# The order of the first loads in a fused attention and rational feed-forward kernel: small transfers set between large ones, two more pieces of the first weight ahead of values and queries

## The chip, the cores and the metric

The kernel runs on one core of a Trainium2 chip. The metric is device time in microseconds (us) of one execution: the median of three runs is compared. Besides, one execution is recorded by the hardware profiler; its times are counted from the start of its span.

## What is computed

Attention through 32 packed queries `p` per head, with 8 batches, 8 heads, 576 rows and a head dimension of 64, and behind it a feed-forward layer with a rational activation, all in 32-bit floats, the weights coming in as 64-bit floats:

```python
p_packed = sm_attn(p, k, v)                 # softmax(p k^T / 8) v, 32 rows for a head
out      = sm_attn(q, p_packed, p_packed)   # softmax(q p_packed^T / 8) p_packed
x = out.transpose(0, 2, 1, 3).reshape(4608, 512)
h = x @ w_in                                # 512 x 2048
P = a0 + a1*h + a2*h**2 + a3*h**3
Q = 1 + |b0|*|h| + |b1|*h**2
result = (P / (Q + 1e-6)) @ w_out           # 2048 x 512
```

## The kernel before

**Weights as words.** `w_in` and `w_out` are 64-bit floats, handed over as 64-bit integers. They come in 16 pieces of 1 MB, which the kernel calls words: eight of `w_in` and eight of `w_out`, each made of 256 of the 2048 inner columns (or rows). Each word is loaded by two transfers of 512 KB. The list `words` (line 369) holds them in the order in which they fall due: words 0 to 5 are of `w_in`, word 6 is the first of `w_out`, and from there the two kinds alternate. `load_words(n)` (line 380) issues loads until n words lie loaded and not yet converted, as far as buffers are free; a word lies in one of the buffers `m0` to `m3` or `w1` to `w5`. `w2` and `w3` hold values and queries of batch 0 first and are given to words only once the variable `started` is set. `convert()` (line 431) makes 32-bit floats of the next word: two activations on ScalarE (profile: `m<-m` and `win<-m`, or `w<-w` and `win<-w`) and three instructions on VectorE (TENSOR_SCALAR, SCALAR_TENSOR_TENSOR, and an integer addition that the profile calls CUSTOM_DVE_ANT_0 and the list of instructions ISA), each on 128 x 1024 elements. A converted word of `w_in` lies in `win`.

**Loads of a batch.** `load(bb, what)` (line 468) issues the transfers of batch `bb`. For batch 0 they are `k0`, `k1`, `v0`, `v1`, `q0` and `q1` of 512 KB each, one half of the heads' first 512 rows, into the tiles `nat` (keys) and `w2`, `w3` (values, queries), and `rem`, all that is small: the keys' last 64 rows (tile `AH`, 128 KB in rows of 256 bytes), the packed queries (`pn`, four transfers of 16 KB, and a copy of them on GpSimd), the queries' last 64 rows (also `AH`, two of 64 KB) and the values' last 64 rows (`rv`, two of 64 KB). All are issued on SyncE's queue. The four coefficients `a` and two `b` go to the tile `ab` from `constants()` (line 337); from them VectorE computes the tiles `root` and `abS`, and ScalarE loads four registers from `abS` (TENSOR_LOAD).

**Attention of one batch.** `attention(bb)` (line 539) transposes the keys on TensorE (copied to the tile `kx` by ScalarE), takes the packed queries' scores, reduces their maxima on VectorE, exponentiates on ScalarE, transposes the result, multiplies by the values into the tile `acc` (profile, batch 0: `acc<-w,kx` and `acc<-rv,small`), scales that on VectorE (`small<-acc,small`), transposes it to `ppT`, and then lets the queries attend to it. Its output goes to `AH` and `AL`, the high and low parts of a split that lets TensorE keep 32-bit accuracy in three passes.

**Feed-forward.** `m_chunk` multiplies a converted piece of `w_in` by `ppT` ahead of time, so that `hidden` works on attention weights of 128 columns; `hidden(bb, x, c)` computes one unit of h, the rational function (tiles `U`, `V`, `Y` on ScalarE, VectorE and GpSimd) and `gh`, `gl`; `acc_block` multiplies by `w_out` and sums in `acc`. There are 128 units; the first 12 use `w_out` undivided, while words are still being converted.

**What sets the order.** Every call is recorded and not issued: the class `Planner` (line 32) collects the operations, finds their dependencies, and lays them out by list scheduling with a table of costs (a transfer is costed by its size and the length of its contiguous runs). `pin()` gives everything recorded so far the first ranks in the order of recording, so the loads before `nc.pin()` stay as written on SyncE's queue. The order of the other engines is what the planner makes of the whole. `issue` then emits each engine's instructions in that order, and each engine works through its own in order. Where the plan has TensorE idle, `idle` puts multiplications by zero in between (`acc<-w,zero`, profile line 223). All other instructions carry line 226 in the profile, so they are told apart by their tiles.

The lines that the change touches are those of `load` under `what == "rem"` and the start of the program:

```python
load_words(3)
for what in ("k0", "rem", "k1", "v0", "v1", "q0", "q1"):
    load(0, what)
nc.pin()
constants()
```

Of the kernel before, what the change touches and what calls it, by code (L numbers as in the profile page):

```python
# [257 lines left out]
def attention_rational_ffn(  # L258
# [18 lines left out]
    REM = T - NS * P  # L277
# [6 lines left out]
    HREM = REM // 2  # L284
# [35 lines left out]
    pn_ring = Ring(sb, "pn", 1, [P, NG, 2, D])  # L320

    rv_ring = Ring(sb, "rv", 1, [P, H // 2, D])
# [57 lines left out]
    def load_words(n):  # L380
        while len(words_in) < min(len(words), converted + n):
            r = len(words_in)
            kind, i, n2 = words[r]
            used = [x for x, _ in words_in]
            free = [x for x, end in room if r < end and x not in used[converted:]]
            free = [x for x in free if x[0] is not w_ring or x[1] not in (2, 3) or started]
            if not free:
                return
            x = min(free, key=lambda x: max((j for j in range(r) if used[j] == x), default=-1))
            raw = x[0].at(x[1], [P, n2 * 512], I64)  # L390
            if kind == "in":
                c = i // 2
                for y in range(2):
                    src = w_in[2 * y * P : (2 * y + 2) * P, c * CF : (c + 1) * CF].rearrange("(x p) f -> p x f", p=P)
                    nc.sync.dma_start(raw[:, 512 * y : 512 * (y + 1)].rearrange("p (x y) -> p x y", x=2), src)
            else:
                for y in range(n2):
                    nc.sync.dma_start(raw[:, 512 * y : 512 * (y + 1)], w_out[(i + y) * P : (i + y + 1) * P, :])
            words_in.append((x, raw))
# [65 lines left out]
    NAT, AH, AL, PPT = {}, {}, {}, {}  # L465
    rows4 = lambda bb: bb < 2

    def load(bb, what):
        if bb >= B:
            return  # L470
        if what == "rem":

            rv, pn = NAT[bb, "rv"], NAT[bb, "p"] = rv_ring.next(), pn_ring.next()
            if rows4(bb):
                r = NAT[bb, "r"] = AH_ring.at(bb, [P, H, D], F32)
                nc.sync.dma_start(r[0:REM], k[bb, :, NS * P : T, :].rearrange("h p d -> p h d"))
            for j in range(NJ):
                src = p[bb, NG * j : NG * j + NG].rearrange("r n d -> n r d")
                nc.sync.dma_start(pn[32 * j : 32 * j + 32, :, 0, :], src)
            nc.gpsimd.tensor_copy(pn[:, :, 1, :], pn[:, :, 0, :])  # L480
            for i in range(2 if rows4(bb) else 0):
                src = q[bb, 4 * i : 4 * i + 4, NS * P : T, :].rearrange("h (p x) d -> p h (x d)", x=2)
                r2 = r[REM + HREM * i : REM + HREM * (i + 1)].rearrange("p (h x) d -> p h (x d)", x=2)
                nc.sync.dma_start(r2, src)
            for i in range(2):
                src = v[bb, 4 * i : 4 * i + 4, NS * P : T, :]
                if rows4(bb):
                    nc.sync.dma_start(rv[REM * i : REM * (i + 1)], src.rearrange("h p d -> p h d"))
                    continue
                for y in range(2):  # L490
                    o = REM * i + HREM * y
                    nc.sync.dma_start(rv[o : o + HREM], src.rearrange("h (p y) d -> y p h d", y=2)[y])
            return
        x, g = what[0], int(what[1])
        src = {"k": k, "q": q, "v": v}[x][bb, 4 * g : 4 * g + 4]
        if not rows4(bb):
            t = NAT[bb, what] = nat_ring.next()
            if x == "v":
                t = NAT[bb, what] = t[:, 0 : 4 * NS * D].rearrange("p (h s d) -> p h s d", h=4, s=NS)
                for y in range(2):  # L500
                    to = t.rearrange("p h (y i) d -> p h y (i d)", y=2)[:, :, y]
                    nc.sync.dma_start(to, src[:, 2 * P * y : 2 * P * (y + 1)].rearrange("h (p i) d -> p h (i d)", i=2))
                return
            src = src.rearrange("h t d -> (h t) d")
            for i in range(2):
                for y in range(2):
                    o = 64 * i + 32 * y
                    blocks = src[:, 32 * y : 32 * y + 32].rearrange("(a t i) d -> i t a d", t=32, i=2)[i]
                    nc.sync.dma_start(t[o : o + 32].rearrange("p (a d) -> p a d", d=32), blocks)
            return  # L510
        src = src[:, 0 : NS * P, :]
        if bb == 0 and x != "k":
            if g == 0:
                NAT[x] = w_ring.at(2 + "vq".index(x), [P, 2, 4 * NS * D], F32)
            t = NAT[x][:, g, :]
        else:
            t = nat_ring.next()[:, 0 : 4 * NS * D]
        t = t.rearrange("p (h s d) -> p h s d", h=4, s=NS)
        nc.sync.dma_start(t, src.rearrange("h (p s) d -> p h s d", s=NS))
        NAT[bb, what] = t  # L520
# [18 lines left out]
    def attention(bb):  # L539
# [34 lines left out]
        for g in range(2):  # L574
            transposed("k", g)
            if bb > 0:
                load(bb, f"v{g}")
            yield
# [130 lines left out]
        if bb > 0:  # L709
            load(bb, "q0")  # L710
            load(bb, "q1")
# [196 lines left out]
        elif i == 1:  # L908
            nc.sync.dma_start(ov, o)

    load_words(3)
    for what in ("k0", "rem", "k1", "v0", "v1", "q0", "q1"):
        load(0, what)
    nc.pin()
    constants()
    for _ in attention(0):
# [9 lines left out]
    mt, fill, rem = {}, {}, {}  # L926
# [100 lines left out]
```

## Time and profile before

| | |
|---|---|
| median of 3 runs (lowest to highest) | 794.99 us (794.15 to 795.89) |
| the profiled execution, its own time | 795.3 us |
| its span, first to last instruction | 793.2 us |
| granted TensorE clock, mean over the span | 0.975 |
| TensorE busy (matmuls) | 751.6 us, 95% |
| VectorE busy | 698.0 us, 88% |
| ScalarE busy | 662.4 us, 84% |
| GpSimd busy | 453.3 us, 57% |
| moved by DMA | 56.05 MB in 152028 packets |

The profile names TensorE's matmuls PE, its weight loads PEld, VectorE DVE, ScalarE ACT, GpSimd POOL and SyncE's queue SPq. A row of the timeline has the start in us, the length in us, the engine, the line, the operation, the tiles as output<-inputs without buffer numbers, the shapes, the count, and in brackets how long the engine was idle just before and whom it waited for. A row of the stretches has, for each engine, its busy time and in brackets its instructions, then the granted clock of TensorE, the share of the 16 DMA engines and the GB/s. A row of the chain of waits has the start, the length and what the end of the program hung on at that time. A row of the DMA view has the output<-input, the queue, the count, the size of each and the time from issue to landing.

### The profile page before, as it was taken

To read this page: it belongs to the slowest core of one execution; us is meant where nothing else is said; L and a number is where in the kernel's file an instruction comes from. 1 tells how busy PE (TensorE), PEld (TensorE's weight loads), DVE (VectorE), ACT (ScalarE), POOL (GpSimd) and SP (SyncE) were. 2 spreads that over 40 slices of the span, in tenths; PEclk is the share of its full clock that TensorE was granted. 3 is DMA by queue.
4 is the path that set the end of the run, shared out by engine and by line. 5 is a ranking of instruction groups with operands and counts; after the bars stand their busy time and mean duration, and the time that the engine had idled before them with its cause. 6 is when DMAs were issued, how large, how long until landed. Compare 5 with 4: busy or idle time off the path is not lost.

```text
span 793.2 us, 15205 instructions
## 1 busy us (share of the span) xinstructions
PE 751.6 (95%) x5452; PEld 578.9 (73%) x5452; DVE 698.0 (88%) x1298; ACT 662.4 (84%) x1482; POOL 453.3 (57%) x448
## 2 busy tenths in 40 slices
PE   2759999999999999999999999999999999999997
PEld 1436655588778887678777887678777887778886
DVE  4698999998999889998999789998999789998873
ACT  5788979998888888889798798889798798998872
POOL 0012357657576646756587556755587455856663
PEclk9757999999999999999999999999999999999999
DMA  8974326022901038021901138011901122000001
GB/s 268 347 254 162 136 61 87 1 58 49 105 28 54 31 54 114 1 57 43 113 28 52 43 42 116 1 58 46 108 28 50 36 44 56 1 9 20 27 1 41
DMA packets 152028, 56.05 MB, mean 71 GB/s; under 512 B 122256, under 2 KB 141200, under 8 KB 151952
## 3 DMA queue, kind: packets, MB, share of 16 engines
q1 hardware_dynamic: 151952, 55.07, 30.9%
q8 instruction: 43, 0.70, 0.4%
q14 instruction: 33, 0.27, 0.1%
HBM read 45.62 MB, written 9.44 MB: 69 GB/s over the span
## 4 chain that ended last, share of the span: by engine, by line
PE 76%; DVE 10%; ACT 10%; DMA 2%; issue 2%; SPq 1%; POOL 0%; DVEq 0%; ACTq 0%
PE acc L226 38%; PE h L226 23%; PE at L226 14%; DVE Y L226 5%; DVE w L226 2%; ACT Y L226 2%; ACT U L226 1%; DMA AH<-in_k_dram 1%; ACT m L226 1%; ACT kx L226 1%; ACT V L226 1%; ACT sq L226 1%; DVE small L226 1%; DVE V L226 1%; ACT w L226 1%
## 5 line engine op out<-in xcount | busy, mean ns | idle before, releaser
L226 POOL TENSOR_TENSOR U<-U,sq 128x576 f32<-128x576 f32 x128 | 184.9, 1445 | 117.9 <-ACT U L226 54.6
L226 PE MATMUL acc<-w,gh 128*128 128x512 f32 x736 | 237.6, 408 | 1.5 <-ACT gh L226 1.0
L226 PE MATMUL h<-AH,m 128*128 128x288 f32 x1024 | 191.9, 308 | 9.6 <-DVE Y L226 6.9
L226 PEld LDWEIGHTS h<-AH,m 128*128 128x128 f32 x1024 | 158.8, 191 | 41.5 <-DVE Y L226 22.6
L226 POOL TENSOR_TENSOR gl<-Y,gh 128x512 fp32r<-128x512 f32 x116 | 150.1, 1294 | 43.3 <-issue 18.0
L226 PEld LDWEIGHTS acc<-w,gh 128*128 128x128 f32 x736 | 132.1, 188 | 44.8 <-issue 12.2
L226 PE MATMUL acc<-w,gl 128*128 128x512 f32 x384 | 148.1, 413 | 0.7 <-DVE gl L226 0.7
L226 ACT ACTIVATE Y<-h,abS 128x288 f32<-128x288 f32 x256 | 125.9, 507 | 23.1 <-PE h L226 18.9
L226 ACT ACTIVATE sq<-h 128x288 f32<-128x288 f32 x256 | 106.1, 416 | 38.5 <-PE h L226 32.0
L226 DVE TENSOR_TENSOR Y<-Y,h 128x288 f32<-128x288 f32 x256 | 109.6, 446 | 26.0 <-ACT Y L226 9.0
L226 DVE SCALAR_TENSOR_TENSOR Y<-Y,abS,h 128x288 f32<-128x288 f32 x256 | 124.8, 506 | 2.3
L226 DVE SCALAR_TENSOR_TENSOR Y<-Y,abS,V 128x576 f32<-128x576 f32 x128 | 102.9, 804 | 24.1 <-ACT V L226 23.9
L226 PE MATMUL h<-AL,m 128*128 128x288 f32 x512 | 111.0, 298 | 0.0
L226 ACT ACTIVATE U<-h 128x288 f32<-128x288 f32 x256 | 98.3, 419 | 11.5 <-DVE V L226 6.7
L226 ACT ACTIVATE V<-U,one 128x576 f32<-128x576 f32 x128 | 97.9, 765 | 4.8 <-DVE Y L226 4.2
L226 DVE SCALAR_TENSOR_TENSOR V<-U,V 128x576 f32<-128x576 f32 x128 | 96.2, 752 | 0.0
L226 DVE SCALAR_TENSOR_TENSOR Y<-V,Y 128x576 f32<-128x576 f32 x116 | 86.7, 748 | 1.8
L226 PEld LDWEIGHTS acc<-w,gl 128*128 128x128 f32 x384 | 71.5, 188 | 22.7 <-issue 8.8
L226 ACT ACTIVATE V<-V 128x576 f32<-128x576 f32 x128 | 84.2, 658 | 0.6
L226 PEld LDWEIGHTS h<-AL,m 128*128 128x128 f32 x512 | 83.2, 190 | 0.6 <-issue 0.4
L226 POOL COPY G<-Y 128x64 f32<-128x64 f32 x116 | 27.5, 237 | 97.6 <-DVE Y L226 87.0
L226 PE MATMUL acc<-half,gh 128*128 128x512 f32 x240 | 78.6, 414 | 1.1 <-ACT gh L226 1.1
(137 smaller groups left out, 1020.0 us busy)
## 6 DMA issues: line engine op xcount, KB each, us to landing
w<-in_moe_w_out_dram SPq DMA_DIRECT2D x16, 512.0 KB, 4.5
out_dram<-half SPq DMA_DIRECT2D x15, 512.0 KB, 3.1
nat<-in_k_dram SPq DMA_DIRECT2D x48, 144.0 KB, 3.9
nat<-in_q_dram SPq DMA_DIRECT2D x48, 144.0 KB, 4.4
nat<-in_v_dram SPq DMA_DIRECT2D x24, 256.0 KB, 3.4
m<-in_moe_w_in_dram SPq DMA_DIRECT2D x8, 512.0 KB, 6.7
w<-in_moe_w_in_dram SPq DMA_DIRECT2D x8, 512.0 KB, 8.6
nat<-in_k_dram SPq DMA_DIRECT2D x4, 512.0 KB, 10.0
```

What stands on the lines that cost most here:

```text
L226: getattr(getattr(self.nc, engine), name)(*args, **kwargs)
```

## The change

The branch for `rem` in `load` is cut in four, which can be called by themselves: `r` (the keys' last rows), `p` (packed queries with their copy), `qr` (the queries' last rows) and `rv` (the values' last rows). Called as `rem`, for batches 1 to 7, the four go out one after the other; there the two tiles `rv` and `pn` are now made at their own parts. For batch 0 the order is now written as one list, in which a number n stands for `load_words(n)`: words 0 and 1, `r`, word 2, `p`, `k0`, `k1`, `qr`, word 3, `rv`, `v0`, `v1`, word 4, `q0`, `q1`. Before, it was words 0, 1 and 2, `k0`, all of `rem`, `k1`, `v0`, `v1`, `q0`, `q1`, and words 3 and 4 came behind, together with the coefficients. The code behind the loop, `load_words(6)` among it, stands as it was.

```diff
         if what == "rem":
-
-            rv, pn = NAT[bb, "rv"], NAT[bb, "p"] = rv_ring.next(), pn_ring.next()
+            for x in ("r", "p", "qr", "rv"):
+                load(bb, x)
+            return
+
+        if what == "r":
             if rows4(bb):
                 r = NAT[bb, "r"] = AH_ring.at(bb, [P, H, D], F32)
                 nc.sync.dma_start(r[0:REM], k[bb, :, NS * P : T, :].rearrange("h p d -> p h d"))
+            return
+        if what == "p":
+            pn = NAT[bb, "p"] = pn_ring.next()
             for j in range(NJ):
...
             nc.gpsimd.tensor_copy(pn[:, :, 1, :], pn[:, :, 0, :])
+            return
+        if what == "qr":
             for i in range(2 if rows4(bb) else 0):
...
                 nc.sync.dma_start(r2, src)
+            return
+        if what == "rv":
+            rv = NAT[bb, "rv"] = rv_ring.next()
             for i in range(2):
...
-    load_words(3)
-    for what in ("k0", "rem", "k1", "v0", "v1", "q0", "q1"):
-        load(0, what)
+    for what in (2, "r", 3, "p", "k0", "k1", "qr", 4, "rv", "v0", "v1", 5, "q0", "q1"):
+        if isinstance(what, int):
+            load_words(what)
+        else:
+            load(0, what)
     nc.pin()
```

What it moves is seen in the engines' instructions. On SyncE's queue, at the start of the program, stood this before (`m_1` to `m_3` are words 0 to 2, `m_4` and `w_3_119` words 3 and 4; `AH` holds `r` and `qr`, `w_1_84` the values and `w_2_85` the queries):

```order
L226 DMA m_3_78<-in_moe_w_in_dram 128x2x256 x2
L226 DMA nat_1_79<-in_k_dram 128x4x256
L226 DMA AH_1_82<-in_k_dram 64x8x64
L226 DMA pn_1_81<-in_p_dram 32x2x64 x4
L226 DMA AH_1_82<-in_q_dram 32x4x128 x2
L226 DMA rv_1_80<-in_v_dram 64x4x64 x2
L226 DMA nat_2_83<-in_k_dram 128x4x256
L226 DMA w_1_84<-in_v_dram 128x4x256 x2
L226 DMA w_2_85<-in_q_dram 128x4x256 x2
L226 DMA ab<-in_moe_b_dram 128x2
L226 DMA m_4_118<-in_moe_w_in_dram 128x2x256 x2
...
L226 DMA w_3_119<-in_moe_w_in_dram 128x2x256 x2
```

At the same place of SyncE's queue stands now (`m_3_79` is word 2, `m_4_83` word 3 and `w_2_86` word 4, `w_1_85` the values, `w_3_87` the queries):

```order
L226 DMA AH_1_78<-in_k_dram 64x8x64
L226 DMA m_3_79<-in_moe_w_in_dram 128x2x256 x2
L226 DMA pn_1_80<-in_p_dram 32x2x64 x4
L226 DMA nat_1_81<-in_k_dram 128x4x256
L226 DMA nat_2_82<-in_k_dram 128x4x256
L226 DMA AH_1_78<-in_q_dram 32x4x128 x2
L226 DMA m_4_83<-in_moe_w_in_dram 128x2x256 x2
L226 DMA rv_1_84<-in_v_dram 64x4x64 x2
L226 DMA w_1_85<-in_v_dram 128x4x256 x2
L226 DMA w_2_86<-in_moe_w_in_dram 128x2x256 x2
L226 DMA w_3_87<-in_q_dram 128x4x256 x2
L226 DMA ab<-in_moe_b_dram 128x2
```

The nine small transfers (one, four, two and two) no longer stand in a row between `k0` and `k1`; two words, four large transfers, have moved ahead of the queries, and one of the two ahead of the values.

On VectorE, in batch 0's attention, stood this before, from the scaling of the product with the values (`small<-acc`) to the conversion of word 3 (`m_4`):

```order
L226 TENSOR_SCALAR abS<-root 128x1
L226 SCALAR_TENSOR_TENSOR abS<-abS 128x2
L226 TENSOR_SCALAR small<-acc_7_101,small 128x128
L226 SCALAR_TENSOR_TENSOR small<-acc_7_101,small 128x128
L226 TENSOR_SCALAR m_4_118<-m_4_118 128x1024
L226 SCALAR_TENSOR_TENSOR m_4_118<-m_4_118 128x1024
L226 ISA win<-m_4_118,win 128x2048
L226 STREAM_TRANSPOSE kx_1_86<-at_10_114 128x288
```

On VectorE, at the same place of the attention, stands now (`m_4_83` is word 3, `w_2_86` word 4):

```order
L226 TENSOR_SCALAR m_4_83<-m_4_83 128x1024
L226 SCALAR_TENSOR_TENSOR m_4_83<-m_4_83 128x1024
L226 TENSOR_SCALAR small<-acc_7_103,small 128x128
L226 ISA win<-m_4_83,win 128x2048
L226 SCALAR_TENSOR_TENSOR small<-acc_7_103,small 128x128
L226 TENSOR_SCALAR w_2_86<-w_2_86 128x1024
...
L226 SCALAR_TENSOR_TENSOR w_2_86<-w_2_86 128x1024
L226 TENSOR_SCALAR root<-root 128x1
L226 SCALAR_TENSOR_TENSOR abS<-abS 128x2
L226 ISA win<-w_2_86,win 128x2048
...
L226 STREAM_TRANSPOSE kx_1_88<-at_10_116 128x288
```

The conversion of word 3 has moved ahead of and in between the scaling, and that of word 4 ahead of the transposes of the queries' scores; the work on `root` and `abS` has moved behind the scaling.

On ScalarE, from the last copy of the scores' operands on, the words' activations have moved in between the attention's own instructions. Before:

```order
L226 ACTIVATE kx_1_86,small<-at_4_95,small 128x320
...
L226 ACTIVATE small<-small 128x4
L226 COPY kx_1_86<-acc_6_98 128x512
L226 COPY kx_1_86<-at_6_99 128x512
...
L226 ACTIVATE root<-root 128x1 x2
L226 ACTIVATE m_4_118<-m_4_118 128x1024
L226 COPY kx_1_86<-acc_8_102 128x2x256
L226 ACTIVATE win<-m_4_118 128x1024
```

And now on ScalarE (`m_4_83` is word 3, `w_2_86` word 4, `kx<-acc_8` the first copy of transposed queries):

```order
L226 ACTIVATE m_4_83<-m_4_83 128x1024
L226 ACTIVATE kx_1_88,small<-at_4_97,small 128x320
...
L226 ACTIVATE small<-small 128x4
L226 COPY kx_1_88<-acc_6_100 128x512
L226 ACTIVATE win<-m_4_83 128x1024
L226 COPY kx_1_88<-at_6_101 128x512
...
L226 ACTIVATE w_2_86<-w_2_86 128x1024
L226 ACTIVATE win<-w_2_86 128x1024
L226 COPY kx_1_88<-acc_8_104 128x2x256
```

Word 3's first activation now stands ahead of the exponentials, and both of word 4's ahead of the first copy of the queries. Of the multiplications by zero there are now 26 in place of 30. Behind what runs at some 340 us in the trace of before, the instructions of all engines stand in the same order as before.

More of the change, by code (lines that the diff above doesn't have):

```diff
@@ L480, in load @@
             nc.gpsimd.tensor_copy(pn[:, :, 1, :], pn[:, :, 0, :])
+            return
+        if what == "qr":
             for i in range(2 if rows4(bb) else 0):
                 src = q[bb, 4 * i : 4 * i + 4, NS * P : T, :].rearrange("h (p x) d -> p h (x d)", x=2)
-                r2 = r[REM + HREM * i : REM + HREM * (i + 1)].rearrange("p (h x) d -> p h (x d)", x=2)
+                r2 = NAT[bb, "r"][REM + HREM * i : REM + HREM * (i + 1)].rearrange("p (h x) d -> p h (x d)", x=2)
                 nc.sync.dma_start(r2, src)
+            return
+        if what == "rv":
+            rv = NAT[bb, "rv"] = rv_ring.next()
             for i in range(2):
```

## The prediction

> **What bounds the kernel now.** I read the stretches first, then the chain of waits, then the engines' timelines up to 60 us. The stretches from the start (us; busy time of PE, PEld, DVE, ACT, POOL, then granted clock, DMA share, GB/s):
>
> ```profile
> 10.00:20.00 10.00, 4.90 (x30) 3.60 (x30) 7.39 (x8) 5.58 (x9) 0.30 (x1) 1.00 0.87 237
> 20.00:30.00 10.00, 8.00 (x111) 5.12 (x112) 4.48 (x24) 5.42 (x16) 0.00 (x0) 0.50 0.98 338
> 30.00:40.00 10.00, 7.06 (x98) 3.89 (x94) 8.24 (x15) 8.81 (x15) 0.00 (x0) 0.99 1.07 349
> 40.00:60.00 20.00, 12.28 (x62) 7.87 (x62) 19.17 (x29) 17.33 (x31) 2.13 (x2) 0.51 0.74 249
> 60.00:80.00 20.00, 18.76 (x127) 13.00 (x126) 17.68 (x28) 18.23 (x43) 4.26 (x3) 0.80 0.49 175
> 80.00:119.00 39.00, 37.92 (x326) 23.15 (x325) 39.00 (x67) 33.55 (x72) 17.94 (x12) 1.00 0.28 92
> 119.00:200.00 81.00, 80.70 (x594) 57.07 (x595) 75.36 (x152) 73.57 (x167) 54.61 (x52) 1.00 0.29 51
> ```
>
> From 80 to 119 us DVE has no idle time at all; from 119 us on PE has next to none. The chain of waits has the hand-over:
>
> ```profile
> 117.52 1.13 DVE w L226
> 118.64 0.61 DVE gh L226
> 119.26 0.04 issue
> 119.30 1.98 PE acc L226 x4
> ```
>
> So the time is DVE's start, up to the last converted word at 118.6 us, and TensorE's work behind it. DVE's work in the first stage is the same before and after (the same conversions, the same first attention). What the change can win is DVE's idle time before 119 us: 2.6 us in the second row, 5.5 in the third, 1.8 in the fourth, 0.8 in the fifth, 2.3 in the sixth. Up to 33 us it lies in these rows of DVE's timeline (brackets: idle just before, and whom it waited for):
>
> ```profile
> 16.33 1.23 DVE L226 CUSTOM_DVE_ANT_0 win<-m,win 128x2048 uint16<-128x2048 uint16 x1
> 21.72 0.42 DVE L226 TENSOR_REDUCE small<-acc 128x1 f32<-128x256 f32 x1 [4.16 <-PE acc L226]
> ...
> 25.45 0.16 DVE L226 SCALAR_TENSOR_TENSOR root<-ab 128x1 f32<-128x1 f32 x1 [1.12 <-DMA ab<-in_moe_b_dram]
> 28.32 0.16 DVE L226 RECIPROCAL root<-root 128x1 f32<-128x1 f32 x1 [1.17 <-ACT root L226]
> 30.85 0.35 DVE L226 TENSOR_SCALAR small<-acc,small 128x128 f32<-128x128 f32 x1 [1.56 <-PE acc L226]
> 32.06 0.35 DVE L226 TENSOR_SCALAR small<-acc,small 128x128 f32<-128x128 f32 x1 [0.48 <-PE acc L226]
> 32.86 0.69 DVE L226 TENSOR_SCALAR m<-m 128x1024 int32<-128x1024 int32 x1
> 33.59 1.23 DVE L226 SCALAR_TENSOR_TENSOR m<-m 128x1024 int32<-128x1024 int32 x1
> 34.85 1.23 DVE L226 CUSTOM_DVE_ANT_0 win<-m,win 128x2048 uint16<-128x2048 uint16 x1
> ```
>
> Five waits, 8.5 us. Word 2 is done at 17.6 us and word 3 not begun until 32.9: between them DVE only follows the attention. Why the attention is late stands in the chain, and why the transfer it waits for is late in SyncE's queue (the two `rv`) and in the DMA rate from 0 to 60 us (40 slices of 1.5 us):
>
> ```profile
> 4.46 9.40 DMA AH<-in_k_dram
> 13.86 0.02 issue
> 13.88 0.60 SPq L226
> ...
> 14.52 4.15 DMA nat<-in_k_dram
> ```
> ```profile
> 12.97 1.50 SPq L226 DMA_DIRECT2D rv<-in_v_dram  x2
> ```
> ```profile
> GB/s 0 169 384 395 396 396 384 346 188 51 77 311 366 354 348 347 319 333 259 411 395 411 400 390 351 290 144 30 117 393 359 333 373 399 378 188 0 227 401 71
> ```
>
> The second `rv`, the 16th transfer, goes out at 13.88, when `r`, the 8th, has landed at 13.86: a transfer waits until the one eight places before it has landed. With nine small ones in a row, eight places hold little work, so the rate falls to 188, 51 and 77 GB/s from 12 to 16.5 us, and `k1` goes out at 14.52 and lands at 18.67. The scores need all keys.
>
> **The change part by part.** *The transfers.* At the row's 384 to 396 GB/s (mean 390) 512 KB take 1.35 us. Five landings, each from a view of its own short stretch (last column: from issue to landing; issues at 3.92 for `k0`, from 15.17 for `v`, 16.27 for `q`, 18.82 for word 3, 20.59 for word 4):
>
> ```profile
> nat<-in_k_dram SPq DMA_DIRECT2D x1, 512.0 KB, 9.0
> w<-in_v_dram SPq DMA_DIRECT2D x2, 512.0 KB, 5.5
> w<-in_q_dram SPq DMA_DIRECT2D x2, 512.0 KB, 7.4
> m<-in_moe_w_in_dram SPq DMA_DIRECT2D x2, 512.0 KB, 8.3
> w<-in_moe_w_in_dram SPq DMA_DIRECT2D x2, 512.0 KB, 10.2
> ```
>
> `k0` lands at 12.9 and `r` 0.9 behind it: 0.9 us is the price of `r`. Before, the small ones took from 12.9 to about 16 us; I take 0.9 for `r`, 0.8 for `p`, 0.4 for `qr`, 0.6 for `rv`. Now no eight transfers in a row are small, so I let the stream run on. Words 1 and 2 landed when ScalarE began them:
>
> ```profile
> 8.63 1.21 ACT L226 ACTIVATE m<-m 128x1024 f32<-128x1024 f32 x1 [0.57 <-DMA m<-in_moe_w_in_dram]
> 11.36 1.19 ACT L226 ACTIVATE m<-m 128x1024 f32<-128x1024 f32 x1 [0.52 <-DMA m<-in_moe_w_in_dram]
> ```
>
> Word 1's landing, 8.6, stays. From there: `r` 9.5, word 2 12.2 (11.3 before), `p` 13.0, `k0` 14.4, `k1` 15.9, `qr` 16.3, word 3 19.0, `rv` 19.6, `v` 22.4, word 4 25.1, `q` 27.9. Against before: `k1` 2.8 us earlier; word 3 some 8.5 and word 4 some 7 us earlier; the second half of `v` 0.7 later (16 + 5.5 = 21.7 before) and of `q` 3.4 later (17 + 7.4 = about 24.5).
>
> *A page on this rate.* The Trainium skill, "DMA: Bandwidth & Descriptors", Specifications, gives a core about 358 GB/s from HBM. By it a large transfer takes 1.46 us, `k1` lands 0.45 us later and the sum below is smaller by that. The rows up to 10.5 us lie above it, at up to 396 GB/s, so the measurement decides.
>
> *Idle time before the first reduction.* The reduction began 3.05 us behind `k1` (18.67 to 21.72). Now the copies of packed queries and last keys stand behind `k1`'s copies on ScalarE and not ahead of them, two copies of this kind:
>
> ```profile
> 16.82 0.37 ACT L226 COPY kx<-at 128x256 f32<-128x256 f32 x1 [0.48 <-PE at L226]
> ```
>
> So it begins at 15.9 + 3.05 + 0.75 = 19.7, 2.0 us earlier. DVE ends word 2 as before: its activations now end at 12.2 + 2.2 = 14.4, when DVE is free for it (16.33 less the two instructions ahead). The wait is 2.1 in place of 4.2.
>
> *The waits behind it.* The last exponential, of 128 x 4, stood at 25.45 and now at 23.45, its result 0.2 later; DVE has nothing else from 24.3 - 2.0 = 22.3 on, so it waits some 1.3 us (1.1 before). It does 0.6 us of sums and then wants word 3, whose second activation stands behind a copy of 0.6 us on ScalarE:
>
> ```profile
> 25.45 0.22 ACT L226 ACTIVATE small<-small 128x4 f32<-128x4 f32 x1
> 25.86 0.59 ACT L226 COPY kx<-acc 128x512 f32<-128x512 f32 x1 [0.20 <-PE acc L226]
> 27.09 0.59 ACT L226 COPY kx<-at 128x512 f32<-128x512 f32 x1 [0.64 <-PE at L226]
> ...
> 28.19 1.14 ACT L226 ACTIVATE m<-m 128x1024 f32<-128x1024 f32 x1
> ```
>
> Copy at 23.9, activation 24.5 to 25.6: DVE waits 1.2 us, from 24.3. The first two instructions of word 3 take it to 27.4. The same activation holds the second copy up to 25.6 (27.09 - 2.0 = 25.1 without it), so the product with the values ends 1.9 us earlier than before, at 28.9, and DVE waits 1.5 us for it. The waits for `root` (1.2) and for the second scaling (0.5) go: word 3's rest and word 4 stand in between. Sum: 2.1 + 1.3 + 1.2 + 1.5 = 6.1 in place of 8.5, **2.4 us won**. As a check, the transposes of the queries' scores begin when pT and the words ahead of them are done, at 35.5 to 36 (36.3 before), with one word more converted, which is 0.69 + 1.23 + 1.23 = 3.1 us of work, and 0.5 of `root` left over.
>
> *Behind that.* The fifth stretch's 0.8 us lies here:
>
> ```profile
> 49.37 0.76 DVE L226 TENSOR_TENSOR AL<-kx,AH 128x576 fp32r<-128x576 f32 x1 [0.54 <-ACT AH L226]
> 50.41 0.70 DVE L226 TENSOR_SCALAR w<-w 128x1024 int32<-128x1024 int32 x1 [0.29 <-ACT win L226]
> ```
>
> Both wait for ScalarE, which ran a word's activation ahead of the copy to `AH`. Now that word stands behind the first copy, and ScalarE has one word less to do here. I take these **0.8 us as won**; the bounds are 0 and 0.8. The 2.3 us from 60 to 80 us, mostly waits for ScalarE's U and V, I leave where they are; bounds -2.3 and +1, what one more word's activation in the way costs.
>
> *What hides the later ones.* `q` lands at 27.9 and TensorE takes it up behind the product with the values, at 28.9 at the earliest: 1 us of cover. `v` has 3.6 (22.4 to 26.0), word 4 1.3 on ScalarE. Once cover is gone each microsecond costs one, since all stand in order. The coefficients land some 4 us later (b 25.4 before); DVE asks for them only behind the scaling, at about 31. POOL's copy of `pn`, 0.3 us, moves with `p` on an engine that is idle there. The SP issues number the same; the four fewer multiplications by zero lie where PE waits.
>
> Sum: -2.4 - 0.8 = **-3.2 us**. From 119 us on, now 116, nothing is added or taken, and the order differs little. The profiled execution, 795.3 us with a span of 793.2, lies 0.3 above the median; it would become 792.1, the median 794.99 - 3.2 = **791.8 us**. About 0.2%, 1.6 us, is what a measurement of this kernel can tell.
>
> **The rivals.** *The words close the later gaps too* (0.16): ScalarE, relieved of two words, no longer holds DVE from 60 to 80 us. -3.2 - 2.3 = -5.5: 789.5. For it: its share there is 18.23 of 20, DVE's waits are for it. Against: it has the same work for the units.
>
> *ScalarE takes over* (0.20): DVE is ahead, ScalarE less so, because two words now stand between the attention's copies and it waits there for the coefficients (TENSOR_LOAD ahead of a copy). It gains about 1.6 us up to 36 us (one word's two activations, 2.1, less `root`, 0.45), and the waits from 60 to 80 us grow by what DVE is ahead. -0.5 to -1.6, say 793.9: mostly no change.
>
> *The queries come late* (0.09), slower: the stream doesn't hold 390 GB/s. At the 237 GB/s of 10 to 20 us a large transfer takes 2.2 us: `k1`, four of them on, lands at 19.3, so with the two copies the product with the values ends 1.4 us later than before, at 32.2; `q`, twelve on, lands at 38.1, and TensorE, ScalarE and DVE, all in order, stand 5.9 us there, of which word 3, already converted, gives back 3.1: +4.2, 799.2. It decides from about 280 GB/s down (1.9 us each: product at 31.0, `q` at 34.5, 0.2 + 3.5 - 3.1 = +0.6). Against it: 338 and 349 GB/s from 20 to 40 us, with eight transfers out.
>
> *The stall was not the row of small ones* and `k1` is as late as before: then 2 of the 3.2 us go, -1.2, within the second rival's range and chance.
>
> **How the numbers follow.** Forecast 0.55, rivals 0.16, 0.20 and 0.09. Faster: 0.55 + 0.16 + a quarter of 0.20 = 0.76; same 0.15; slower 0.09. The range reaches to the first rival and 0.8 beyond for a differing order up to 340 us, 788.7, and to the weak end of the second, 794.5; outside are the slower rival and the tails.
>
> **What would show it.** Right: no dip under 250 GB/s before 25 us; `k1` within 0.7 us of 15.9; DVE's first reduction at 19 to 20.5; word 3's DVE work before 30; the hand-over to PE at 115 to 117. Wrong: a wait of PE for `w<-in_q_dram` of over 1 us; DVE idle over 3.5 us from 60 to 80; a hand-over at 118 or later.

## The result and the profile after

The changed kernel takes 788.96 us (median of 6 runs, 787.65 to 790.89), the kernel before in the same comparison 795.63 us (6 runs, 794.15 to 796.23). The medians differ by 6.7 us, where the forecast was 3.2; the recorded ratio is 0.9922, with a 95% interval of 0.9903 to 0.9941. Two later comparisons of the same two kernels gave 6.1 us (0.9907, 0.9887 to 0.9927) and 6.3 us (0.9916, 0.9900 to 0.9932). Here and below microseconds are differences of medians; the ratio in brackets with its interval is the recorded one, and it isn't always the ratio of the medians (0.9923 where 0.9907 is recorded). The result lies in the forecast range of 788.7 to 794.5 us, 0.3 us from its fast end.

The profiled execution of after took 790.89 us, span 788.8 us, and is the slowest of its six. Against the span before, 793.2 us, it is 4.4 us shorter; what follows on it explains those 4.4 us, and a faster execution comes with the experiments. Its stretches (columns as before: PE, PEld, DVE, ACT, POOL, clock, DMA share, GB/s):

```profile
10.00:20.00 10.00, 4.87 (x30) 4.27 (x38) 7.62 (x8) 6.34 (x10) 0.88 (x1) 1.00 1.10 323
20.00:30.00 10.00, 6.65 (x156) 5.09 (x145) 6.93 (x18) 9.12 (x21) 0.00 (x0) 1.00 1.09 357
30.00:40.00 10.00, 5.71 (x74) 2.23 (x72) 9.71 (x28) 8.02 (x17) 0.00 (x0) 0.98 0.90 294
40.00:60.00 20.00, 13.20 (x70) 9.73 (x70) 16.24 (x27) 14.82 (x31) 2.13 (x2) 0.50 0.64 209
60.00:80.00 20.00, 18.42 (x128) 11.45 (x126) 18.51 (x31) 18.56 (x41) 5.48 (x4) 0.91 0.55 180
```

DVE's idle time from 10 to 40 us fell from 9.9 to 5.7 us; from 40 to 60 us it rose from 0.8 to 3.8; from 60 to 80 us it fell from 2.3 to 1.5. From 80 to 119 us DVE is again busy throughout. The DMA rate in 40 slices of the first 60 us no longer has the hole from 12 to 16.5 us (188, 51 and 77 GB/s before); its lowest slice from 3 to 25 us is the eleventh, 231:

```profile
GB/s 0 149 392 393 399 257 300 359 306 351 231 354 336 301 351 373 386 353 334 365 392 418 373 350 298 106 26 122 389 350 304 328 395 391 234 22 0 0 0 246
```

TensorE takes up the second half of the keys as it lands (first row, TensorE's timeline), at 16.9 us in place of 18.7. On DVE's timeline four waits are left up to 33 us, 4.9 us in all, and the product with the values (27.75) is there when DVE asks for it; but 2.0 us of waiting are new at 52.6 us:

```profile
16.93 1.12 PE L226 MATMUL acc<-ident,nat 128*128 128x128 f32 x4 [0.33 <-DMA nat<-in_k_dram]
```
```profile
15.19 0.70 DVE L226 TENSOR_SCALAR m<-m 128x1024 int32<-128x1024 int32 x1 [0.62 <-ACT win L226]
...
20.60 0.42 DVE L226 TENSOR_REDUCE small<-acc 128x1 f32<-128x256 f32 x1 [2.19 <-PE acc L226]
...
24.18 0.16 DVE L226 TENSOR_TENSOR small<-small 128x4 f32<-128x4 f32 x1 [1.36 <-ACT small L226]
...
25.68 0.70 DVE L226 TENSOR_SCALAR m<-m 128x1024 int32<-128x1024 int32 x1 [0.75 <-ACT win L226]
...
27.75 0.35 DVE L226 TENSOR_SCALAR small<-acc,small 128x128 f32<-128x128 f32 x1
...
52.61 0.69 DVE L226 TENSOR_SCALAR w<-w 128x1024 int32<-128x1024 int32 x1 [2.02 <-ACT w L226]
```

The chain of waits shows for whom: word 6, the first of `w_out`. Its first half goes out at 42.25 us and lands 6.9 us later; its second half goes out at 42.8 us and, by the DMA view, lands 7.6 us later, at 50.4, when ScalarE begins on it:

```profile
42.25 6.86 DMA w<-in_moe_w_out_dram
49.11 1.36 issue
50.48 2.10 ACT w L226 x2
```

The hand-over from DVE to PE comes at 117.4 us in place of 119.3:

```profile
114.64 1.57 DVE w L226
116.20 1.16 DVE Y L226 x2
117.36 0.04 issue
117.41 1.07 PE h L226 x6
```

So the hand-over is 1.9 us earlier, and the end 4.4 us. The other 2.5 us lie behind it. The stretches up to and from the hand-over, before:

```profile
0.00:119.30 119.30, 88.92 (x747) 56.63 (x747) 98.47 (x174) 94.01 (x187) 25.63 (x24) 0.84 0.61 204
119.30:793.20 673.90, 662.66 (x4705) 522.26 (x4705) 599.58 (x1126) 568.40 (x1296) 427.69 (x425) 1.00 0.26 47
```

And after:

```profile
0.00:117.41 117.41, 85.61 (x755) 56.31 (x755) 98.52 (x180) 95.87 (x194) 27.91 (x24) 0.90 0.65 208
117.41:788.80 671.39, 659.55 (x4690) 520.16 (x4690) 597.13 (x1119) 566.57 (x1288) 427.17 (x424) 1.00 0.27 47
```

DVE has done the same 98.5 us of work at both hand-overs, so 20.8 us of idle time before and 18.9 after (less 1.9). But PE has 15 fewer matmuls left, 3.1 us of work (less 0.6 us of idle time more, which gives the 2.5). The reason stands in DVE's order: the last instruction on the last word, before, ends at 118.65 us, ahead of the hand-over,

```profile
117.43 1.22 DVE L226 CUSTOM_DVE_ANT_0 w<-w,w 128x2048 uint16<-128x2048 uint16 x1
```

and after, it ends at 119.15 us, 1.7 us behind it:

```profile
117.94 1.21 DVE L226 CUSTOM_DVE_ANT_0 w<-w,w 128x2048 uint16<-128x2048 uint16 x1
```

The new plan sets the last word one unit further back, and DVE does more for the units, TensorE's food, before it. The times at which DVE ends a unit's `Y<-Y,abS,V` (after less before; units counted from 0) are the marks of the units. They show it as a jump: unit 5 is 2.2 us earlier, unit 6 6.9 us. Up to unit 47 the marks swing, from 0.7 us later to 6.9 us earlier; from the 48th to the last they stay at 4.1 to 4.3 us earlier.

Theories for the excess over the forecast: **A**, the data come earlier and DVE idles less than I reckoned; **B**, TensorE's clock: it was at half from 20 to 30 us before and at full speed after, and all of the start runs quicker for it; **C**, the planner's order of the first units, which changed along with the loads.

### The profile page after: what moved, and what is told of

Same layout as the page of the kernel before. It is cut to its first block, busy times and chain, and to the rows that moved or that the text cites. A ratio compares the mean times of both kernels' runs of the same rounds, so it can differ in the third digit from the quotient of the medians.

```text
span 788.8 us, 15182 instructions
## 1 busy us (share of the span) xinstructions
PE 745.2 (94%) x5444; PEld 576.5 (73%) x5444; DVE 695.6 (88%) x1298; ACT 662.4 (84%) x1482; POOL 455.1 (58%) x448
## 4 chain that ended last, share of the span: by engine, by line
PE 73%; DVE 9%; ACT 9%; DMA 4%; issue 1%; SPq 1%; POOL 0%; DVEq 0%; ACTq 0%
PE acc L226 36%; PE h L226 23%; PE at L226 14%; DVE Y L226 5%; DMA m<-in_moe_w_in_dram 2%; ACT Y L226 2%; DVE w L226 2%; ACT U L226 1%; DMA w<-in_moe_w_out_dram 1%; DMA w<-in_moe_w_in_dram 1%; ACT sq L226 1%; ACT V L226 1%; ACT m L226 1%; SPq L226 1%; DVE small L226 1%
## 5 line engine op out<-in xcount | busy, mean ns | idle before, releaser
L226 ACT ACTIVATE Y<-h,abS 128x288 f32<-128x288 f32 x256 | 126.7, 511 | 21.9 <-PE h L226 18.4
L226 ACT ACTIVATE V<-U,one 128x576 f32<-128x576 f32 x128 | 98.5, 769 | 5.7 <-DVE Y L226 4.5
```

What stands on the lines that cost most here:

```text
L226: getattr(getattr(self.nc, engine), name)(*args, **kwargs)
```

## The experiments

Each time stands beside the kernel before, which took 795.55 to 795.76 us in the three comparisons.

**One part alone.** The small transfers set between the large ones, the words left where they were:

```diff
-    for what in (2, "r", 3, "p", "k0", "k1", "qr", 4, "rv", "v0", "v1", 5, "q0", "q1"):
+    for what in (2, "r", 3, "p", "k0", "k1", "qr", "rv", "v0", "v1", "q0", "q1"):
```

> The small transfers alone go between the large ones; words 3 and 4 are loaded where they were before, behind the queries. Theory A (the prediction's: VectorE's idle time shrinks because the keys come earlier and because words 3 and 4 are there to fill it): only the keys' part is left, about 2.0 us faster than before, some 793.6 against 795.6 for before. Theory B (the gain is TensorE's granted clock: with the keys' work and the scores following without a gap the clock stays full from 20 to 30 us and half-clock time falls from 37 to some 24 us): the keys come early here too, so most of the gain stays, 4 to 6 us faster, and the clock over the span is 0.984 or more in place of 0.975.

And the words alone:

```diff
-    for what in (2, "r", 3, "p", "k0", "k1", "qr", 4, "rv", "v0", "v1", 5, "q0", "q1"):
+    for what in (3, "k0", "rem", "k1", 4, "v0", "v1", 5, "q0", "q1"):
```

> Words 3 and 4 alone move ahead of values and queries; the small transfers stand in a row between the two halves of the keys as before. Theory A: the second half of the keys lands at about 18.7 us as before; VectorE has word 3 to fill its first idle time, so about 1.2 us faster than before (794.4), at most 3. Theory B: TensorE waits between the two halves of the keys as before, the clock falls to half at 20 us, and the kernel is within 1 us of before, clock about 0.975.

Measured: 793.73 us (0.9975, 0.9962 to 0.9987), 1.9 us faster, for the small ones, and 792.82 us (0.9964, 0.9952 to 0.9975), 2.8 us faster, for the words, though the keys are as late there as before (19.3 us, 18.7 before). The keys' part is as forecast (2.0), the words' part is more than twice the 1.2 us that I had for it. B's 4 to 6 us for the small ones don't come, and the clock of that profiled execution is 0.976 over the span, where B had 0.984 or more. The run with the words alone leaves B open: its clock is not half from 20 to 30 us, as B expected, but full from 20 to 40 us, and 0.989 over the span.

**The clock.** Multiplications by zero, into a bank that nothing reads yet, wherever the plan has TensorE idle up to the first multiplication by `w_in`; the same edit in before and in after:

```diff
+        cold = cold and not any(str(c[1][0].tensor.tag)[:1] == "h" for c in nc.ops[i][1])
+        if cold and n > 0:
+            z = zero.bitcast(F32)
+            return [("matmul", (warm[0:D, 0:96], z, ident[:, 0:96]), dict(start=True, stop=True, skip_group_check=True))] * ((n + 1) // 2)
```

> The kernel before, with additional multiplications by zero in TensorE's planned idle time up to the first unit of the feed-forward part (into a bank that isn't used yet), so that the clock is held full there; loads as before. Theory A: TensorE isn't what is waited for except for the scores and the product with the values, so 0 to 1.5 us faster than before. Theory B: the clock alone brings 4 us or more, the clock over the span rises to 0.985 or above.

> The changed kernel with the same additional multiplications by zero. Theory A: the same as the changed kernel within 1 us (788 to 791), since VectorE and ScalarE set the pace up to 112 us. Theory B: the changed kernel loses time to half clock from 39.6 to 60 us; held full until the first unit at 48 us it is 2 us or more faster than the changed kernel, and its runs no longer spread over 3 us.

Measured: 796.42 us for before (1.0008, 0.9996 to 1.0020) and 789.67 us for after (0.9919, 0.9903 to 0.9935), which is after's own time. In the warmed kernel before, the clock up to its hand-over is 0.92 in place of 0.84, above after's 0.90, and the hand-over is no earlier (122.4 us in this execution, the slowest of its eleven):

```profile
0.00:122.44 122.44, 96.28 (x850) 64.64 (x850) 98.70 (x173) 93.78 (x187) 25.68 (x24) 0.92 0.59 199
```

The warmed after says nothing on B, since its clock up to the hand-over is 0.88 in the profiled execution, no higher than after's own. But two kernels that come further down add to it: before's order with after's loads, and before's start with after's units, both run at full clock from 20 to 30 us and at 0.89 up to the hand-over, and neither is faster than before (796.57 and 796.03 us). B falls as the cause of the gain: DVE bounds this part, and the higher clock brought nothing in three kernels.

**Loads and orders apart.** SyncE's first 27 transfers can be issued in one kernel's order while every other engine keeps the other's. After's instructions with before's loads:

```diff
-        for i in self.order():
+        order = self.order()
+        first = "m0 m0 m1 m1 m2 m2 nat0 AH0 pn0 pn0 pn0 pn0 AH0 AH0 rv0 rv0 nat1 w2 w2 w3 w3 ab m3 m3 ab w1 w1".split()
...
+        for i in (named[t].pop(0) for t in first):
+            for name, args, kwargs in self.ops[i][1]:
+                getattr(self.nc.sync, name)(*args, **kwargs)
+        for i in order:
+            if i in loads:
+                continue
```

> All engines run the changed kernel's order of instructions, but SyncE issues the first 27 transfers in the order of before (small ones in a row, words 3 and 4 behind the queries). Theory A, earlier data fill VectorE's idle time: the instructions of words 3 and 4 now stand in the queues ahead of work whose data are there sooner, and wait: ScalarE's first activation of word 3, ahead of the exponentials, waits until word 3 lands at about 28 us, so the whole attention comes later; 1 to 6 us slower than before, 797 to 802 us. Theory C, the excess over the forecast (after is 6.7 us faster, 3.2 forecast) comes from the planner putting the last words' conversions behind more units, wherever the data come: the 2 to 4 us of it are kept against the delay, so the time is 794 to 797 us, and the shift of the units' marks jumps by some 3 to 4 us at unit 6 as it does in after.

And before's instructions with after's loads (the same edit in before, with the other list):

> All engines run before's order of instructions, but SyncE issues the first 27 transfers in the changed kernel's order. The keys come earlier, as in the run with the small transfers alone (1.9 us faster), and words 3 and 4 lie ready, but nothing in the queues makes use of them earlier. Theory A: 1.5 to 2.5 us faster than before, about 793.5 us, the marks of the units shifted by a constant -2 from unit 1 on. Theory C says the same of this run; it differs from A in the other. A third view, that the order of the loads by itself is all of it (the instructions' order doesn't matter): 789 us, as after.

Measured: 797.52 us (1.0018, 1.0006 to 1.0031) for the first, 2.0 us slower than before. ScalarE's first activation of word 3 waits for its late word and holds the exponentials, as A had it, and DVE waits 6.3 us for them:

```profile
27.99 1.10 ACT L238 ACTIVATE m<-m 128x1024 f32<-128x1024 f32 x1 [5.64 <-DMA m<-in_moe_w_in_dram]
29.00 0.51 ACT L238 ACTIVATE kx<-at,small 128x320 f32<-128x320 f32 x1
```
```profile
31.15 0.17 DVE L238 TENSOR_TENSOR small<-small 128x4 f32<-128x4 f32 x1 [6.27 <-ACT small L238]
```

Yet the rest behind the hand-over is nearly as short as in after (the table below): 4.3 us more idle time than before, only 2.1 us longer. And the marks jump at unit 6, from 3.6 us later than before to 1.0 us earlier, as C had it.

The second took 796.57 us (1.0010, 0.9996 to 1.0025), no gain, where A and C both had 2 us; its marks have no jump, but stand 0.9 to 1.1 us later than before and not 2 us earlier. I took the coefficients for the cause: they land at 29.2 us there and not at 25.4, and in before's order the work on them stands ahead of the scaling:

```profile
29.22 0.16 DVE L238 SCALAR_TENSOR_TENSOR root<-ab 128x1 f32<-128x1 f32 x1 [3.76 <-DMA ab<-in_moe_b_dram]
```

So the same kernel again, with the coefficients ahead of the values:

```diff
-        first = "m0 m0 m1 m1 AH0 m2 m2 pn0 pn0 pn0 pn0 nat0 nat1 AH0 AH0 m3 m3 rv0 rv0 w2 w2 w1 w1 w3 w3 ab ab".split()
+        first = "m0 m0 m1 m1 AH0 m2 m2 pn0 pn0 pn0 pn0 nat0 nat1 AH0 AH0 m3 m3 rv0 rv0 ab ab w2 w2 w1 w1 w3 w3".split()
```

> Before's order of instructions with the changed kernel's loads, as in the run that gave 796.6 us, but the two transfers of the coefficients stand ahead of the values and not behind the queries. Theory: that run lost its gain because VectorE waited 3.8 us for the coefficients, which land at 29.2 us in place of 25.4 while the work on them stands ahead of the scaling; with them early the keys' gain of about 2 us shows, 793.5 us, and VectorE's wait for the coefficients is under 0.5 us. Rival: the later queries (29.0 us in place of 24.7) hold it as well: 796 us, and TensorE waits for the queries.

Measured: 796.07 us (1.0000, 0.9987 to 1.0012). The wait for the coefficients is gone, and still nothing is won: my cause was not the whole one, and though the rival had the time right (796), its wait of TensorE for the queries isn't there either. TensorE's own order shows why the early keys aren't taken up. The second `acc<-ident,nat` is the half of the keys that now lands at about 16 us. In before's order it stands behind the packed queries, the last keys and their scores, and begins at 18.82 us:

```profile
16.07 0.66 PE L238 MATMUL acc<-ident,pn 128*128 128x128 f32 x2
16.90 1.09 PE L238 MATMUL at<-ident,AH 128*128 128x128 f32 x4 [0.18 <-ACT kx L238]
18.45 0.44 PE L238 MATMUL acc<-kx,small 64*32 64x64 f32 x8 [0.46 <-ACT kx L238]
18.82 1.11 PE L238 MATMUL acc<-ident,nat 128*128 128x128 f32 x4
```

In before that row is this one, at 18.72 us and waiting for its transfer:

```profile
18.72 0.66 PE L226 MATMUL acc<-ident,nat 128*128 128x128 f32 x4 [1.15 <-DMA nat<-in_k_dram]
```

The keys come earlier, the first half and what stands behind it later (word 2 and `r` went ahead), and in an order made for the old arrivals the scores are no earlier: DVE's first reduction stands at 22.5 us, 21.7 in before. The transposes of the queries' scores do begin 0.5 us earlier than before (35.8 us); that goes into waits from 60 to 80 us, with 3.5 us of idle time in place of 2.3.

**The start and the units apart.** All engines follow one kernel's order for what the plan begins in the first 50 us, and from there on the other's; the order is written out as a list of 6954 operations. After's start, before's units:

```diff
-        for i in self.order():
+        self.order()
+        order = [int(x, 36) for x in ORDER.split()]
...
+        for i in order:
```

> The changed kernel with its loads and its order of instructions for all that the plan begins in the first 50 us (the first attention, words 0 to 4); from there on all engines go by before's order of instructions. Theory A (earlier data, VectorE less idle, is all of the gain): 789 to 790 us, as after. Theory C (some 2.2 us of the gain come from the planner's new order of the first units, which puts the last words' conversions behind more units): the 2.2 us go, 791 to 792 us, and in the marks of the units the jump at unit 6 is missing.

And before's start with after's units (the same edit in before, with its own list), beside after itself:

> The kernel before with its loads and its order for all that the plan begins in the first 50 us; from there on all engines go by the changed kernel's order. Theory A: nothing arrives earlier, so 795 to 796 us, as before. Theory C: the order of the units alone brings 2.2 us: 793 to 794 us, with the jump of some 4 us at the mark of unit 6, as in after.

> The changed kernel, unchanged, beside the other three on the same chip: both theories 788 to 790 us; it shows by how much the time of the same instructions differs from run to run.

> The changed kernel, unchanged, as a measure for the first two: 788 to 790 us by every theory.

Measured: 793.83 us (0.9982, 0.9969 to 0.9995) for the first, 1.9 us faster than before; 796.03 us (1.0005, 0.9994 to 1.0016) for the second; 789.46 and 789.42 us for after. So the start alone brings 1.9 us, the units' order alone nothing, and both together 6.1 to 6.7 us. For the first kernel both theories had a larger gain; for the second A had the time, and C didn't. The parts don't add up, and neither theory has that. C's sign came all the same: before's start with after's units has the jump (3.6 us later at unit 5, 1.1 us earlier at unit 6), after's start with before's units has none (1.7 us earlier at both). The profiled executions say why the times don't follow (hand-over from the chain, DVE's busy time from the stretch up to it; idle is the hand-over less the busy time, the rest is the span less the hand-over):

| kernel | DVE busy up to the hand-over | DVE idle | hand-over | rest | span |
|---|---|---|---|---|---|
| before | 98.5 | 20.8 | 119.3 | 673.9 | 793.2 |
| before, warmed | 98.7 | 23.7 | 122.4 | 673.8 | 796.2 |
| before's order, after's loads | 98.5 | 21.7 | 120.2 | 674.0 | 794.2 |
| the same, coefficients early | 98.6 | 21.4 | 120.0 | 674.3 | 794.3 |
| after's start, before's units | 98.2 | 19.4 | 117.6 | 674.2 | 791.8 |
| after | 98.5 | 18.9 | 117.4 | 671.4 | 788.8 |
| after, again | 98.6 | 18.0 | 116.6 | 671.7 | 788.3 |
| after, a third time | 98.3 | 15.9 | 114.2 | 671.4 | 785.6 |
| after, warmed | 98.4 | 18.4 | 116.8 | 671.4 | 788.2 |
| after's order, before's loads | 98.1 | 25.1 | 123.3 | 672.0 | 795.3 |
| before's start, after's units | 99.1 | 24.1 | 123.2 | 672.0 | 795.2 |

DVE's work is the same in all, 98 to 99 us. The rest is 674 us with before's units and 671.4 to 672 us with after's, whatever the start, and PE has 4705 matmuls left in each of the five rows with before's units and 4690 in each of the six with after's. C's 2.0 to 2.5 us are real and come with that order alone. But each order of the units idles more on the other's start. The idle time of one row holds chance too: word 1, which the same first four transfers bring in every kernel, is taken up by ScalarE at 8.6 us in before and at up to 11.1 us in others (the warmed after), so a difference of 1 or 2 us between two rows says little by itself. With after's early start, before's order waits 2.0 us for ScalarE's V (second row, DVE's timeline), and its idle time from 60 to 80 us is 4.0 us:

```profile
60.00:80.00 20.00, 18.66 (x133) 13.04 (x133) 16.00 (x27) 18.01 (x41) 4.27 (x3) 0.83 0.56 200
```
```profile
70.52 0.82 DVE L497 SCALAR_TENSOR_TENSOR Y<-Y,abS,V 128x576 f32<-128x576 f32 x1 [2.01 <-ACT V L497]
```

After's order has 1.5 us of idle time there, and in its third execution, the fastest profiled, next to none:

```profile
40.00:60.00 20.00, 13.61 (x78) 9.87 (x74) 18.37 (x30) 17.13 (x37) 3.36 (x3) 0.57 0.70 240
60.00:80.00 20.00, 19.39 (x148) 12.45 (x147) 19.95 (x34) 19.88 (x46) 4.94 (x4) 1.00 0.61 196
```

With before's late start, after's order idles 24.1 us up to the hand-over (20.8 in before), and the 1.9 us behind it go into that. About half of the 3.3 us more can only be chance: 1.6 us stand ahead of the transposes of the queries' scores (38.1 us), where that kernel has before's loads and order; there word 1 is taken up at 10.4 us and not at 8.6. This profiled execution, 797.06 us, is 1.0 us above its median. The other half stands behind, and is what this execution shows of after's order on that start.

**Word 6 earlier.** After, with the list of buffers turned round, so that word 6 goes into a buffer that is free at once:

```diff
-    room += [((w_ring, i), len(words)) for i in (1, 2, 3)]
     room += [((w_ring, i), index["out", 2 * UNDIVIDED[i][0]]) for i in (4, 5)]
+    room += [((w_ring, i), len(words)) for i in (1, 2, 3)]
```

> After, with the list of free buffers turned round, so that words 5 and 6 (the last loaded before the first units) go into the buffers that are free at once, right behind the coefficients, and words 7 and 8 into those that values and queries free. In after word 6 is issued at 42 us, when the values' buffer is free, and lands at 50.4; VectorE waits 2.0 us for its conversion. Theory A: word 6 lands at about 36 us, VectorE's wait of 2.0 us at 52 us goes, 1 to 2 us faster than after: 787 to 788 us. Rival: the words behind come later in its place and the wait moves to word 7 or 8: no change to after, 789 us.

Measured: 789.07 us (0.9908, 0.9892 to 0.9925), after's time, as the rival had it. (In after it is not the values' buffer that holds word 6, as the expectation says. It goes into the queries' buffer, which TensorE has read by 32.3 us, but in SyncE's queue it stands behind the loads of batch 1 and behind word 5, which goes out only at 39.9 us.) The 2.0 us wait is gone from its trace, but the wait for word 7 or 8 that the rival named doesn't stand in its place; DVE waits 1.3 us for a copy to `AH`, where after has 0.4. From 10 to 40 us DVE idles 7.1 us, and 5.7, 6.6 and 6.4 in after's three executions. Its span of 787.5 us lies among theirs (785.6 to 788.8), so what became of the 2.0 us can't be read from one execution. In after's third execution, with the same instructions as after, that wait is 0.3 us by itself, word 6 landing at 48.7 in place of 50.4 us. No version beat after.

## Why the prediction was right and wrong, step by step

- **The row of small ones delayed the keys.** Right. The hole in the DMA rate is gone, and the small transfers alone bring 1.9 us for a term of 2.0. The keys landed at 16.9, not 15.9 us: their first half at 14.5 (14.4 in the forecast), the second 2.4 us behind it and not 1.5. "I let the stream run on" is what failed here: `k1`, the 13th transfer, went out at 10.24 us after SyncE had waited 0.8 us for `r`, the 5th, so the small ones still took up places among the eight; `k1` then came in the slice of 231 GB/s. The Trainium skill's cap of 358 GB/s for a core ("DMA: Bandwidth & Descriptors", Specifications) is not what did it: slices of after reach 399 and 418 GB/s, and where the keys lost their microsecond the rate was far below the cap.
- **The waits up to 33 us, 6.1 us in place of 8.5.** Right in kind and too high: 4.9 us, so 3.6 won and not 2.4. The first two are as forecast, 2.2 (2.1) and 1.4 (1.3); that for word 3's activation is 0.75 (1.2), 0.6 us stand at word 2, and the 1.5 us for the product with the values are not there: it was done by 27.7, not at 28.9 us. From 10 to 40 us 4.2 us of idle time went in all.
- **The 0.8 us of the fifth stretch, taken as won.** Wrong: there are 3.8 us of idle time (2.9 and 1.6 in the other two executions), above all for word 6. I looked at the words that move ahead, and not at word 6 behind them, which stands in SyncE's queue behind the loads of batch 1 and goes out only at 42 us.
- **The 2.3 us from 60 to 80 us, left where they are.** Too low: 1.5, 0.7 and 0.05 us in three executions. This is the first rival's mechanism, and its time, 789.5, is the nearest; but it needs the new order of the units, since with before's the same start makes those waits grow to 4.0 us. That is the second rival, ScalarE takes over, and its 793.9 is what after's start with before's units took (793.8).
- **The sum for DVE's idle time, -3.2 us.** In three executions -1.9, -2.8 and -4.9 against before's one, mean -3.2. That the mean meets the sum is luck: the terms' errors cancelled.
- **"From 119 us on, now 116, nothing is added or taken, and the order differs little."** This step failed, and it is where the runs show most of the gain beyond the 3.2 us. Nothing is added, but the planner's order of the first units differs enough to put the last word's conversion behind one more unit, so that TensorE has 3.1 us less to do when it takes over: -2.5 us of the -4.4 in the profiled execution, -2.2 and -2.5 in the two others. That the forecast range still holds the result is owed to the 0.8 us that it allowed for a differing order, not to this step.
- **The queries come late.** Didn't happen: TensorE waits for no `w<-in_q_dram`, and the stream held 323 and 357 GB/s.
- **The signs.** Of those named for right, word 3's DVE work came in time (29.2 us, before 30). The others were missed, most of them narrowly: the lowest slice is 231 and not over 250 GB/s, `k1` is 1.0 us from 15.9, the first reduction stands at 20.6, 21.7 and 21.1 us in the three executions (19 to 20.5 named), and the hand-over at 117.4, 116.6 and 114.2, so in one of three between the 115 and 117 named. Of those named for wrong, none came.

Of the 6.1 to 6.7 us between the medians, the three profiled executions of after show 4.4, 4.9 and 7.6 against the one of before. Some 2 to 2.5 us are the order of the units, and the rest is idle time; how much of that is chance can't be told from three executions.

## What to carry to other kernels

Where a planner lays out the whole program, a change of the loads is a change of every engine's order: beside the time of the hand-over to the engine that bounds the rest, compare what that engine has left to do there. Earlier data are worth only what the order behind them asks for; loads moved under a fixed order brought nothing here, and an order moved without its loads cost 2 us. And one profiled execution is a sample: read a term of 1 or 2 us from two or three of them.

## What the runs showed of the hardware

- The same instructions in the same order differ by up to 4.2 us from run to run (786.56 to 790.75 us for after). Two traces of after, 3.4 us apart, place half of that: with the second half of word 6 issued at 42.8 us in both, it lands 7.6 or 5.8 us later, at 50.4 or 48.7 us, which makes 1.7 us of DVE's idle time. Landings at the start differ too: with the same transfers in the same order ScalarE takes up word 1, as it lands, at 8.6 us in before and at 10.4 in before's start with after's units.
- TensorE's granted clock changes in steps of 3.41 us. In after it is at half for 20.48 us on end, six such steps, then at full for one (to 63.46 us) and at half for one (to 66.88):

```profile
39.57:60.05 20.48, 13.31 (x77) 9.73 (x70) 16.72 (x29) 15.30 (x32) 2.13 (x2) 0.50 0.62 205
```

  The Trainium skill ("TensorE: Matmul & The Clock Gate", Part 1) has a free-running window of 3413 ns, and the trace agrees with its length. Where DVE bounds the work, up to the hand-over, raising the clock from 0.84 to 0.92 saved no time that could be measured (0.8 us longer, interval -0.3 to 1.6).
